# Start-up order, a second bank for the first sums of a batch, step pacing, logit order and a plain last product in a fused attention and expert kernel

## The chip, the cores and the metric

The kernel runs on one core of a Trainium2 chip. The metric is the time of one execution on the device, in microseconds (us); the time before is the median of nine runs. The engines are named as the profile names them: PE (matrix products; PEld are its weight loads), DVE (vector), ACT (scalar, with the exponential), POOL and SP; SP, ACT and POOL also issue the DMA transfers.

## The reference

Attention over 4 batches, 8 heads, 768 positions and 64 channels feeds 8 experts. A head is either a full causal one or a streaming one, which sees the first 4 positions and the last 64. The output of the attention, x, has 3072 tokens of 512 channels.

```python
mask = np.where(retr, causal, causal & (is_sink | in_win))
scores = np.where(mask, scale * (q @ k.T), -1e9)
a = softmax(scores)
x = (a @ v).transpose(0, 2, 1, 3).reshape(N, D)       # N, D = 3072, 512
P = np.exp(x @ w_gate - max)                          # N x 8
for _ in range(8):
    P /= P.sum(1, keepdims=True) + 1e-09
    P /= P.sum(0, keepdims=True) + 1e-09
    P *= N / E
out = sum(P[:, e:e + 1] * (np.maximum(x @ w1[e], 0) @ w2[e]) for e in range(8))
```

## The kernel before

**Attention, 0 to 157 us of the profiled execution.** A unit is a batch b, a block g of 256 queries (three in a batch) and a half u of the heads; a unit has two pairs of heads (a = 0, 1). `emit_prep` turns keys and queries of a unit by PE transposes into a PSUM tile "tr", which DVE copies to kT. `emit_scores` makes one chunk of scores (tile "sc", two buffers of two PSUM banks); its two closures are the exponential on ACT (L457, writes PT) and the product with a mask on DVE (L466, L469). A round is two chunks; a batch has 12 rounds: 2 with g = 0, 4 with g = 1, 6 with g = 2. `gen_pv` sums PT times v for one pair in a PSUM tile "pv" of one buffer; `normalize` (L300, L301) divides on DVE and writes xn, after which the buffer is free. `turn` transposes xn into a tile "xt", which ACT copies to xT (L319). All of tr, xt, the values' placement "vp", the logits "lgp" and the steps of expert 0 ("l1", "l2") share the PSUM tag "mo" with three buffers.

**Steps of expert 0 as filling.** Each finished query block adds six steps to the list `fillers`: four of layer 1 (`first_steps`, L355: eight products of 256 columns, counted as 1) and two of layer 2 (L369: eight of 512 columns, counted as 2), 96 counts in all. `finish_sums` puts one step between the two sums of a round, and `spend(n)` at the end of round n takes steps until a target count is reached: (with 48 rounds) 4 + 68 (n - 5) // 42. 72 are done at the last round, the other 24 go between the eight Sinkhorn iterations (L598 to L618, 157 to 181 us).

**Order.** The first six rounds are written out by hand for PE, DVE and ACT (L520 to L575: this order is kept on those engines). They begin with nine products on zeros (`keep_warm`), then `make_far` and `make_keep`, which build flags and masks from is_retrieval, then `round_first`, `emit_prep`, `scores`. After that a scheduler orders the instructions of each engine.

**Logits.** `emit_logits` makes, for a batch, 6 token blocks of 8 columns in one bank, each by four products over the channel quarters (L336), block after block.

**Experts 1 to 7, 181 us to the end.** Works are pairs (e, c) of an expert and one of six chunks of 512 tokens. Both layers use seven products in place of eight (Strassen-Winograd). `combine_h` makes four sums of hidden values for a work on DVE (L648, tile S). `layer2` takes the products in the order 1, 5, 6, 2, 7, 3, 4, each eight matmuls of 256 columns (L780), and adds each product's bank to acc: on DVE (L797) or by ACT and an accumulating DMA (L794, L802). In the last two works all adds are on DVE. `body(n)` interleaves layer 1 of a work with layer 2 of the work before; the last work's layer 2 runs after the loop alone (L858 to L860), with its banks split in halves over more PSUM tiles (`final`). `store` sends a finished quarter of a chunk by two DMAs; in the last chunk one is issued by SP and one by ACT (L761).

Of the kernel before, what the change touches and what calls it, by code (L numbers as in the profile page):

```python
# [36 lines left out]
def kernel(  # L37
# [128 lines left out]
    def round_first(h0):  # L166
# [3 lines left out]
        for i in range(2):  # L170
# [27 lines left out]
    nc.vector.memset(fm, 1.0)  # L198
    nc.vector.memset(wm, 1.0)
    retf = constp.tile([128, H], F32, tag="retf")  # L200
    nc.vector.tensor_copy(
        out=retf, in_=ret_u.rearrange("p (e two) -> p e two", two=2)[:, :, 0]
    )
    over = constp.tile([128, H], F32, tag="over")
    nc.vector.tensor_scalar(out=over, in0=retf, scalar1=-1.0, scalar2=1.0,
                            op0=ALU.mult, op1=ALU.add)
    sinks = [slice(64 * o, 64 * o + (n_sink + 1 - o) // 2) for o in range(2)]
    sinks = [rows for rows in sinks if rows.stop > rows.start]
    masks = [cp.tile([128, 2, 640], F16, tag=f"mask{j}", name=f"mask{j}") for j in range(4)]
# [3 lines left out]
    def make_keep():  # L213
        nc.vector.scalar_tensor_tensor(
            out=keep[:, 256:512], in0=wm, scalar=1.0, in1=fm, op0=ALU.add, op1=ALU.mult)
        nc.vector.tensor_copy(out=keep[:, 0:256], in_=keep[:, 256:512])
        for rows in sinks:
            nc.vector.tensor_scalar(out=keep[rows, 0:256], in0=fm[rows, :], scalar1=2.0,
                                    scalar2=None, op0=ALU.mult)
        nc.vector.tensor_copy(out=keep[:, 512:640], in_=keep[:, 256:384])  # L220
# [9 lines left out]
            )  # L230

    def make_far():

        for i in range(2):
            nc.scalar.activation(out=farf[:, :, i], in_=retf, func=AF.Copy, bias=0.0, scale=1.0)
        for rows in sinks:
            nc.vector.memset(farf[rows, :, 0], 1.0)
        for i in (1, 0):
            spell_far(i, farf[:, :, i].unsqueeze(2).broadcast_to([128, H, DV]))

# [38 lines left out]

    def gen_pv(b, g, u, a, PT, scale):  # L280

        pv = psA.tile([128, 2, 2, DV], F32, tag="pv", bufs=1, name=f"pv_{b}_{g}_{u}_{a}")
        vt, vf = vts[b], vfs.get(b)
        todo = pv_of(g)
        for i, (kj, far, sb, off) in enumerate(todo):
            for hh in range(2):
                nc.tensor.matmul(
                    out=pv[:, sb, hh, 0:D + 1], lhsT=PT[:, hh, off:off + 128],
                    rhs=(vf if far else vt)[:, 4 * u + 2 * a + hh, kj, 0:D + 1],
                    start=(i == 0 and hh == 0), stop=(i == len(todo) - 1 and hh == 1),  # L290
                    skip_group_check=True,
                )
            yield
        if a == 0:
            xns[b, g, u] = ap.tile([128, 2, 2, 2, D], F16, tag="xn", name=f"xn_{b}_{g}_{u}")
        xn = xns[b, g, u]

        def normalize():
            rc = ap.tile([128, 2, 2], F32, tag="rc", bufs=4, name=f"rc_{b}_{g}_{u}_{a}")
            nc.vector.reciprocal(out=rc, in_=pv[:, :, :, D])  # L300
            nc.vector.tensor_tensor(  # L301
                out=xn[:, a], in0=pv[:, :, :, 0:D],
                in1=rc.unsqueeze(3).broadcast_to([128, 2, 2, D]), op=ALU.mult)
            if a == 1:
                turns.append((b, g, u))
        scale.append(normalize)
# [23 lines left out]

    def emit_logits(b):
        lgp = psA.tile([128, 512], F32, tag="mo", bufs=3, name=f"lgp_{b}")
        for i in range(NC):
            nb = b * NC + i
            for dc in range(4):
                nc.tensor.matmul(  # L336
                    out=lgp[:, i * E:(i + 1) * E], lhsT=xT[dc // 2][:, dc % 2, ts(nb, 128)],
                    rhs=wg16[:, dc, :], start=(dc == 0), stop=(dc == 3),
                )
        nc.scalar.activation(  # L340
            out=Pne[:, b * NC:(b + 1) * NC, :],
            in_=lgp[:, 0:NC * E].rearrange("p (n e) -> p n e", e=E),
            func=AF.Exp, bias=0.0, scale=1.0,
        )
# [132 lines left out]
    def fill(n):  # L477

        while n > 0 and fillers:
            done = fillers.pop(0)()  # L480
            n -= done
            left[0] -= done
# [11 lines left out]

    rounds = len(tasks) // 2
    def spend(n):
        fill(left[0] - (92 - 68 * (n - 5) // (rounds - 6)))

    def sum_later(n):
        for i, a, ci in tasks[2 * n:2 * n + 2]:  # L500
# [5 lines left out]
    def scores(n):  # L506
        return [emit_scores(*t) for t in tasks[2 * n:2 * n + 2]]
# [11 lines left out]
    engines = {mybir.EngineType.PE, mybir.EngineType.DVE, mybir.EngineType.Activation}  # L519
    with tc.manual_schedule(engines=engines):  # L520
        keep_warm(blank[:, 0:128], blank, 9)
        make_far()
        make_keep()
        round_first(0)
        emit_prep(*units[0])
        round_first(4)
        r0 = scores(0)
        soften(r0, (0,))
        make_masks((0, 1))
        emit_prep(*preps.pop())  # L530
        warm(3)
        r1 = scores(1)
        soften(r1[:1], (0,))
        place_v(0)
        soften(r0, (1,))
        sum_later(0)
        soften(r1[1:], (0,))
        make_masks((2, 3))
        emit_prep(*preps.pop())
        warm(2)  # L540
        r2 = []
        finish_sums(lambda: r2.extend(scores(2)))
        soften(r1, (1,))
        soften(r2, (0,))
        warm(2)
        turn()
        sum_later(1)
        r3 = scores(3)
        place_v(1)
        finish_sums(lambda: emit_prep(*preps.pop()))  # L550
        soften(r3, (0,))
        emit_vfar(0, 1)
        soften(r2, (1,))
        sum_later(2)
        turn()
        r4 = scores(4)
        finish_sums()
        soften(r3, (1,))
        soften(r4, (0,))
        fill(1)  # L560
        sum_later(3)
        finish_sums()
        soften(r4, (1,))
        fill(1)
        r5 = scores(5)
        turn()
        emit_prep(*preps.pop())
        soften(r5, (0,))
        spell_far(2, farx[:, :, 1])
        sum_later(4)  # L570
        finish_sums()
        fill(1)
        soften(r5, (1,))
        sum_later(5)
        fill(1)  # L575
# [182 lines left out]

    def store(c, i, n):
        for o in range(2):  # L760
            (nc.scalar if c == NCH - 1 and o else nc.sync).dma_start(  # L761
                out=out[ts(c, CH), :].rearrange("(q i p c) (n d) -> i n c p q d", q=2, i=2, c=2, n=2)[i, n, o],
                in_=acc[c][64 * o:64 * o + 64, i, n, :, :],
            )

    def layer2(e, c):
        banks = {}
        final = (e, c) == works[-1]

        def product(k, bank, first, last=False):  # L770
            if first and final:

                banks[bank] = [psB.tile([128, 512], F32, tag="l1" if bank == "y" else "l2",
                                        name=f"l2{bank}{q}")[:, 0:256] for q in range(2)]
            elif first:
                t = psB.tile([128, 2, 256], F32, tag="l2", name=f"l2{bank}")
                banks[bank] = [t[:, q, :] for q in range(2)]
            for q in range(2):
                for f in range(4):
                    nc.tensor.matmul(  # L780
                        out=banks[bank][q], lhsT=lefts2[e, c][k - 1][:, q, f, :],
                        rhs=rights2[e][k - 1][:, f, :],
                        start=(first and (final or q == 0) and f == 0),
                        stop=(last and (final or q == 1) and f == 3), skip_group_check=True,
                    )

        def add(bank, i, n, by_dma):
# [23 lines left out]
        for k in (1, 5, 6, 2, 7, 3, 4):  # L811
# [5 lines left out]
                store(c, i, n)  # L817
            yield

    gens = {name: iter(()) for name in ("l1", "l2", "h", "w", "x", "first")}
# [5 lines left out]
    def body(n):  # L828
        e, c = works[n]
        if c == 0 and e + 1 < E:  # L830
            expw[e + 1] = load_expert(e + 1)
        if c == 2 and e + 1 < E:
            gens["w"] = combine_w(e + 1)
        if e == 1:
            gens["first"] = weight_first(c)
            gens["x"] = combine_x((c + 1) % NCH)
        for slot in range(7):
            go("l1", 2 if n == 0 and slot == 0 else 1)
            if slot in (1, 3):
                go("w")  # L840
                go("x", 2)
            go("l2")
            if slot in (2, 3, 5, 6):
                go("first")
            if slot in (2, 3):
                go("h")
            if n == 0 and slot == 0:
                run(combine_w(1), 9)
        gens["h"] = combine_h(e, c)
        go("h", 2)  # L850
        gens["l2"] = layer2(e, c)
        if n + 1 < len(works):
            gens["l1"] = layer1(*works[n + 1])

    with tc.manual_schedule(engines={mybir.EngineType.DVE}):
        for n in range(len(works)):
            body(n)
        for _ in range(7):  # L858
            go("h")
            go("l2")  # L860


# [33 lines left out]
```

The softmax here doesn't subtract the row's maximum and nothing guards it: scores larger than these inputs give would overflow.

## Time and profile before

| | us |
|---|---|
| median of nine runs (lowest, highest) | 707.29 (706.85, 707.64) |
| the profiled execution | 707.49 |
| its span, first to last instruction | 705.8 |
| PE, busy in the span | 686.2 |
| DVE, busy | 568.3 |
| ACT, busy | 418.0 |
| POOL, busy | 151.4 |

The time of an execution is 1.7 us longer than the span of its instructions. "Busy" counts the union of an engine's instructions; a matmul's record of 128x256 lasts 272 ns, but matmuls overlap and start about 109 ns apart. In the listings a number in brackets is the time that the engine sat idle before the instruction, with what ended the wait.

### The profile page before, as it was taken

What the parts mean: (1) busy time and instruction counts of PE and PEld (TensorE: products, weight loads), DVE (VectorE), ACT (ScalarE), POOL (GpSimd) and SP (SyncE); (2) the same over time, 40 slices, a digit from 0 to 9 for tenths busy, and PEclk for the clock granted to TensorE, in tenths of its full rate; (3) what the DMA queues carried; (4) which work ended last, traced back from release to release, by engine and by line L of the source; (5) the groups of instructions that cost most, each with busy time, mean ns of one, the idle gap of its engine ahead of it and who ended that gap; (6) DMA issues with size and microseconds to landing.
All of it is one profiled execution on the core that took longest, in us unless ns stands there. A gap on an engine that the chain in (4) does not pass through costs nothing. (4 is left out here: it accounts for less than half of the span.)

```text
span 705.8 us, 17059 instructions
## 1 busy us (share of the span) xinstructions
PE 686.2 (97%) x6932; PEld 569.2 (81%) x6932; DVE 568.3 (81%) x1157; ACT 418.0 (59%) x780; POOL 151.4 (21%) x183
## 2 busy tenths in 40 slices
PE   7999999999999999999999999999999999999995
PEld 3666666666588888888888888888888888888884
DVE  6766666757889988898888879887888789877786
ACT  6777777774795555555555555555555555555550
POOL 7432220000012131222212121222212121121210
PEclk8999999999999999999999999999999999999999
DMA  9999592000734378346924594349424944345774
GB/s 178 179 190 104 52 86 27 3 1 1 120 53 73 57 122 132 62 75 107 148 47 75 94 147 76 60 82 164 84 47 76 154 87 76 60 75 111 148 159 123
DMA packets 84223, 65.61 MB, mean 93 GB/s; under 512 B 48304, under 2 KB 64688, under 8 KB 84144
## 3 DMA queue, kind: packets, MB, share of 16 engines
q0 software_dynamic: 74976, 57.17, 58.5%
q1 hardware_dynamic: 7536, 6.30, 3.6%
q10 hardware_dynamic: 1632, 1.05, 0.5%
q8 instruction: 54, 0.88, 0.5%
q14 instruction: 25, 0.20, 0.1%
HBM read 52.45 MB, written 6.29 MB: 83 GB/s over the span
## 5 line engine op out<-in xcount | busy, mean ns | idle before, releaser
L802 POOL DMA_DIRECT2D acc<-add x120 | 101.4, 845 | 381.9 <-ACT add L794 351.4
L720 ACT ACTIVATE R<-l1y 128x512 f32<-128x512 f32 x164 | 98.7, 602 | 127.5 <-PE l1y L711 92.8
L780 PEld LDWEIGHTS <-S 128*128 128x128 f16 x1344 | 131.2, 98 | 17.0 <-DVE S L648 1.2
L711 PEld LDWEIGHTS <-S 128*128 128x128 f16 x1312 | 128.3, 98 | 17.7 <-issue 2.6
L797 DVE SCALAR_TENSOR_TENSOR acc<-l2y,Pne,acc 128x256 f32<-128x256 f32 x256 | 111.2, 475 | 29.8 <-PE l2y L780 29.7
L780 PEld LDWEIGHTS <-hT 128*128 128x128 f16 x1008 | 98.6, 98 | 12.0 <-issue 0.6
L711 PEld LDWEIGHTS <-w 128*128 128x128 f16 x984 | 96.2, 98 | 12.0 <-issue 0.6
L711 PE MATMUL l1y<-T,S 128*128 128x256 f16 x656 | 98.4, 272 | 1.8 <-ACT R L720 1.8
L457 ACT ACTIVATE PT<-sc 128x1024 f16<-128x1024 f32 (+1 forms) x96 | 83.1, 921 | 16.3 <-PE sc L448 15.4
L780 PE MATMUL l2y<-T,S 128*128 128x256 f16 x672 | 87.1, 273 | 0.0
L794 ACT ACTIVATE add<-l2w,Pne 128x256 f32<-128x256 f32 x80 | 33.7, 473 | 66.1 <-PE l2w L780 64.0
L648 DVE TENSOR_TENSOR S<-hT 128x1024 f16<-128x1024 f16 x84 | 57.6, 685 | 17.0 <-ACT hT L750 14.6
L726 DVE CUSTOM_DVE_ANT_0 hT<-l1z,R 128x512 f16<-128x512 f32 x82 | 56.2, 685 | 8.2 <-ACT R L720 8.2
L726 DVE CUSTOM_DVE_ANT_0 hT<-l1w,R 128x512 f16<-128x512 f32 x82 | 56.1, 684 | 4.3 <-PE l1w L711 0.4
L726 DVE CUSTOM_DVE_ANT_0 hT<-l1y,R 128x512 f16<-128x512 f32 x82 | 55.7, 679 | 0.1
L750 ACT ACTIVATE hT<-l1y 128x512 f16<-128x512 f32 x82 | 49.0, 597 | 4.2 <-PE l1y L711 2.8
L720 ACT ACTIVATE R<-l1w 128x512 f32<-128x512 f32 x82 | 49.4, 603 | 0.0
L711 PE MATMUL l1w<-T,S 128*128 128x256 f16 x328 | 49.4, 273 | 0.0
L711 PE MATMUL l1z<-xT,w 128*128 128x256 f16 x328 | 49.4, 273 | 0.0
L711 PE MATMUL l1w<-xT,S 128*128 128x256 f16 x328 | 49.4, 273 | 0.0
L711 PE MATMUL l1y<-T,w 128*128 128x256 f16 x328 | 49.2, 272 | 0.1
L355 PE MATMUL l<-xT,w 128*128 128x256 f16 x384 | 48.4, 272 | 0.8 <-ACT xT L319 0.8
(102 smaller groups left out, 1025.5 us busy)
## 6 DMA issues: line engine op xcount, KB each, us to landing
acc<-add POOLq DMA_DIRECT2D x120, 256.0 KB, 3.4
w<-in_moe_w_dram POOLq DMA_DIRECT2D x16, 1024.0 KB, 10.4
out_dram<-acc SPq DMA_DIRECT2D x44, 128.0 KB, 2.9
k<-in_k_dram POOLq DMA_DIRECT2D x11, 256.0 KB, 8.0
q<-in_q_dram POOLq DMA_DIRECT2D x11, 256.0 KB, 8.7
v<-in_v_dram POOLq DMA_DIRECT2D x12, 192.0 KB, 9.6
acc<-in_v_dram POOLq DMA_DIRECT2D x3, 256.0 KB, 7.7
acc<-in_q_dram ACTq DMA_DIRECT2D x2, 256.0 KB, 5.5
```

What stands on the lines that cost most here:

```text
L355: nc.tensor.matmul(out=l1[:, ts(fb % 2, 256)], lhsT=w1[:, dc, ts(fb, 128)], rhs=xT[dc // 2][:, dc % 2, c0:c0 + 256], start=(dc == 0), stop ...
L457: nc.scalar.activation(out=PT[:, :, c0:c0 + width], in_=sc[:, :, 0:width], func=AF.Exp, bias=0.0, scale=SCALE,)
L648: nc.vector.tensor_tensor(out=out_, in0=a_, in1=b_, op=op)
L711: nc.tensor.matmul(out=banks[g, bank][:, f, :], lhsT=lefts1[e][k - 1][:, dc, ts(2 * g + f, 128)], rhs=rights1[c][k - 1][:, dc, :], start=( ...
L720: nc.scalar.activation(out=R[name], in_=banks[g, bank], func=AF.Copy, bias=0.0, scale=1.0)
L726: nc.vector._custom_dve(TENSOR_ADD_SAT, out=block(g, i, n), in0=banks[g, bank], in1=R[name], s0=65504.0, s1=0.0)
L750: nc.scalar.activation(out=block(g, 1, 0), in_=banks[g, "y"], func=AF.Relu, bias=0.0, scale=1.0)
L780: nc.tensor.matmul(out=banks[bank][q], lhsT=lefts2[e, c][k - 1][:, q, f, :], rhs=rights2[e][k - 1][:, f, :], start=(first and (final or q ...
L794: nc.scalar.activation(out=t[:, q, :], in_=banks[bank][q], func=AF.Copy, bias=0.0, scale=w)
L797: nc.vector.scalar_tensor_tensor(out=dst, in0=banks[bank][q], scalar=w, in1=dst, op0=ALU.mult, op1=ALU.add,)
L802: nc.gpsimd.dma_start(out=acc[c][:, i, n, :, :], in_=t, accum_op=ALU.add)
```

## The change

Five edits in one. (1) Start-up: retf, over and farf are made inside `make_keep`, farf by DVE and not by ACT; `make_keep` comes ahead of `make_far`; the masks are made in three places, earlier; one group of three fillers of the PE's time becomes two (`warm(2)`), a second group of two is gone; the first `place_v` and the first sums are moved ahead of, or away from, `scores(1)` and `scores(2)`. (2) In `gen_pv` the sum of pair a = 1 of a block g = 0 takes a buffer of "mo". (3) `emit_logits` runs over channel quarters outside and blocks inside. (4) `spend` has a lower target for rounds 6 to 11: 5, 6, 7, 8, 9, 10 counts where it was 5, 7, 8, 10, 12, 13; from round 12 it rises by 60 counts in 35 rounds to the same 72. (5) The last work's layer 2 is plain: `layer2_last` makes four token blocks of eight matmuls of 512 columns (the last block in two halves of 256), adds each with one DVE instruction and stores it at once; `combine_h` is not called for this work, and the special banks are gone from `layer2`.

```diff
@@ make_keep (was: retf and over ahead of it, farf in make_far)
         nc.vector.tensor_copy(out=keep[:, 0:256], in_=keep[:, 256:512])
+        nc.vector.tensor_copy(
+            out=retf, in_=ret_u.rearrange("p (e two) -> p e two", two=2)[:, :, 0]
+        )
+        nc.vector.tensor_scalar(out=over, in0=retf, scalar1=-1.0, scalar2=1.0,
+                                op0=ALU.mult, op1=ALU.add)
+        for i in range(2):
+            nc.vector.tensor_copy(out=farf[:, :, i], in_=retf)
+        for rows in sinks:
+            nc.vector.memset(farf[rows, :, 0], 1.0)
@@ make_far
-        for i in range(2):
-            nc.scalar.activation(out=farf[:, :, i], in_=retf, func=AF.Copy, bias=0.0, scale=1.0)
-        for rows in sinks:
-            nc.vector.memset(farf[rows, :, 0], 1.0)
@@ gen_pv
-        pv = psA.tile([128, 2, 2, DV], F32, tag="pv", bufs=1, name=f"pv_{b}_{g}_{u}_{a}")
+        tag, bufs = ("mo", 3) if g == 0 and a == 1 else ("pv", 1)
+        pv = psA.tile([128, 512], F32, tag=tag, bufs=bufs, name=f"pv_{b}_{g}_{u}_{a}")
+        pv = pv[:, 0:4 * DV].rearrange("p (s h d) -> p s h d", s=2, h=2)
@@ emit_logits
-        for i in range(NC):
-            nb = b * NC + i
-            for dc in range(4):
+        for dc in range(4):
+            for i in range(NC):
                 nc.tensor.matmul(
...
-                    rhs=wg16[:, dc, :], start=(dc == 0), stop=(dc == 3),
+                    start=(dc == 0 and i == 0), stop=(dc == 3 and i == NC - 1),
@@ spend
-        fill(left[0] - (92 - 68 * (n - 5) // (rounds - 6)))
+        done = 4 + 8 * (n - 5) // 7 if n < 12 else 12 + 60 * (n - 12) // (rounds - 13)
+        fill(left[0] - (96 - done))
@@ the hand-written order
         keep_warm(blank[:, 0:128], blank, 9)
+        make_keep()
         make_far()
-        make_keep()
         round_first(0)
+        make_masks((0,))
         emit_prep(*units[0])
+        make_masks((1,))
         round_first(4)
         r0 = scores(0)
         soften(r0, (0,))
-        make_masks((0, 1))
+        make_masks((2, 3))
         emit_prep(*preps.pop())
-        warm(3)
-        r1 = scores(1)
-        soften(r1[:1], (0,))
+        warm(2)
         place_v(0)
         soften(r0, (1,))
         sum_later(0)
-        soften(r1[1:], (0,))
-        make_masks((2, 3))
+        r1 = scores(1)
+        soften(r1, (0,))
         emit_prep(*preps.pop())
-        warm(2)
-        r2 = []
-        finish_sums(lambda: r2.extend(scores(2)))
+        finish_sums()
+        r2 = scores(2)
@@ new
+    def layer2_last(e, c):
+        h, w2 = hTs[e, c], expw[e][1]
+        order = (4, 5, 0, 1, 2, 3, 6, 7)
+        for q, i in ((0, 0), (0, 1), (1, 0), (1, 1)):
+            pieces = 1 + (q == 1 and i == 1)
+            for n in range(pieces):
+                width = 512 // pieces
+                t = psB.tile([128, 512], F32, tag="l1" if n else "l2", name=f"last{q}{i}{n}")
...
+                for j, f in enumerate(order):
+                    nc.tensor.matmul(out=t, lhsT=h[:, q, f, ts(i, 128)],
+                                     rhs=w2[:, f, n * width:(n + 1) * width],
+                                     start=(j == 0), stop=(j == 7))
...
+                nc.vector.scalar_tensor_tensor(
+                    out=dst, in0=t.rearrange("p (n d) -> p n d", d=256),
+                    scalar=Pne[:, 4 * c + 2 * q + i, e:e + 1], in1=dst, op0=ALU.mult, op1=ALU.add)
...
+                for o in range(2):
+                    (nc.scalar if o else nc.sync).dma_start(
+                        out=rows[q, i, o][:, cols], in_=acc[c][64 * o:64 * o + 64, i, cols, q, :])
+                yield
@@ body and the loop over works
+        if n + 1 == len(works):
+            gens["l2"] = layer2_last(e, c)
+            return
...
-        for _ in range(7):
-            go("h")
-            go("l2")
+        go("l2", 9)
```

More of the change, by code (lines that the diff above doesn't have):

```diff
@@ L200 @@
     retf = constp.tile([128, H], F32, tag="retf")
-    nc.vector.tensor_copy(
-        out=retf, in_=ret_u.rearrange("p (e two) -> p e two", two=2)[:, :, 0]
-    )
     over = constp.tile([128, H], F32, tag="over")
-    nc.vector.tensor_scalar(out=over, in0=retf, scalar1=-1.0, scalar2=1.0,
-                            op0=ALU.mult, op1=ALU.add)
     sinks = [slice(64 * o, 64 * o + (n_sink + 1 - o) // 2) for o in range(2)]
@@ L332, in emit_logits @@
         lgp = psA.tile([128, 512], F32, tag="mo", bufs=3, name=f"lgp_{b}")
-        for i in range(NC):
-            nb = b * NC + i
-            for dc in range(4):
+        for dc in range(4):
+            for i in range(NC):
                 nc.tensor.matmul(
-                    out=lgp[:, i * E:(i + 1) * E], lhsT=xT[dc // 2][:, dc % 2, ts(nb, 128)],
-                    rhs=wg16[:, dc, :], start=(dc == 0), stop=(dc == 3),
+                    out=lgp[:, i * E:(i + 1) * E],
+                    lhsT=xT[dc // 2][:, dc % 2, ts(b * NC + i, 128)], rhs=wg16[:, dc, :],
+                    start=(dc == 0 and i == 0), stop=(dc == 3 and i == NC - 1),
+                    skip_group_check=True,
                 )
@@ L760, in store @@
         for o in range(2):
-            (nc.scalar if c == NCH - 1 and o else nc.sync).dma_start(
+            nc.sync.dma_start(
                 out=out[ts(c, CH), :].rearrange("(q i p c) (n d) -> i n c p q d", q=2, i=2, c=2, n=2)[i, n, o],
@@ L767, in layer2 @@
         banks = {}
-        final = (e, c) == works[-1]
         def product(k, bank, first, last=False):
[L771 to L775, printed above, removed]
+            if first:
                 t = psB.tile([128, 2, 256], F32, tag="l2", name=f"l2{bank}")
@@ L782, in product @@
                         rhs=rights2[e][k - 1][:, f, :],
-                        start=(first and (final or q == 0) and f == 0),
-                        stop=(last and (final or q == 1) and f == 3), skip_group_check=True,
+                        start=(first and q == 0 and f == 0), stop=(last and q == 1 and f == 3),
+                        skip_group_check=True,
                     )
@@ L818, in layer2 @@
             yield
+    def layer2_last(e, c):
[6 more added lines that the diff above has]
+                t = psB.tile([128, 512], F32, tag="l1" if n else "l2", name=f"last{q}{i}{n}")
+                t = t[:, 0:width]
+                for j, f in enumerate(order):
+                    nc.tensor.matmul(out=t, lhsT=h[:, q, f, ts(i, 128)],
+                                     rhs=w2[:, f, n * width:(n + 1) * width],
+                                     start=(j == 0), stop=(j == 7))
+                cols = slice(n, n + 1) if pieces == 2 else slice(0, 2)
+                dst = acc[c][:, i, cols, q, :]
+                nc.vector.scalar_tensor_tensor(
+                    out=dst, in0=t.rearrange("p (n d) -> p n d", d=256),
+                    scalar=Pne[:, 4 * c + 2 * q + i, e:e + 1], in1=dst, op0=ALU.mult, op1=ALU.add)
+                rows = out[ts(c, CH), :].rearrange("(q i p c) (n d) -> q i c p n d", q=2, i=2, c=2, n=2)
+                for o in range(2):
+                    (nc.scalar if o else nc.sync).dma_start(
+                        out=rows[q, i, o][:, cols], in_=acc[c][64 * o:64 * o + 64, i, cols, q, :])
+                yield
     gens = {name: iter(()) for name in ("l1", "l2", "h", "w", "x", "first")}
@@ L851, in body @@
         gens["l2"] = layer2(e, c)
-        if n + 1 < len(works):
-            gens["l1"] = layer1(*works[n + 1])
+        gens["l1"] = layer1(*works[n + 1])
     with tc.manual_schedule(engines={mybir.EngineType.DVE}):
```

## The prediction

> **What bounds the kernel now.** I read the page first, then the waits of PE, the timeline at both ends, and windows by stage.
>
> ```profile
> span 705.8 us, 17059 instructions
> PE 686.2 (97%) x6932; PEld 569.2 (81%) x6932; DVE 568.3 (81%) x1157; ACT 418.0 (59%) x780; POOL 151.4 (21%) x183
> ...
> 0.00:10.00 10.00, 5.29 (x33) 2.22 (x33) 5.14 (x18) 4.97 (x10) 8.62 (x17) 0.88 0.97 160
> 10.00:20.00 10.00, 9.38 (x121) 5.16 (x117) 8.05 (x22) 7.73 (x12) 4.95 (x6) 0.78 1.47 197
> 29.00:53.00 24.00, 22.70 (x321) 14.51 (x317) 15.19 (x37) 18.11 (x25) 9.83 (x11) 1.00 1.92 180
> 181.00:691.60 510.60, 508.78 (x4620) 451.63 (x4619) 438.13 (x822) 292.49 (x600) 109.89 (x130) 1.00 0.56 96
> 691.60:705.80 14.20, 6.87 (x58) 5.30 (x56) 9.04 (x21) 0.00 (x0) 0.00 (x0) 0.94 0.43 115
> ```
>
> The window rows give length, then busy time of PE, PEld, DVE, ACT and POOL, then granted clock and DMA. PE is the bound: in 181 to 691.6 us it idles 1.8 us. Its 19.6 idle us lie at the two ends (4.7 and 7.3) and in waits of the attention. The change can gain only there, since its PE work stays nearly the same. The waits, and the end:
>
> ```profile
> PE l L355 <- ACT xT L319: 0.8, 1, 0.8
> PE pv L287 <- DVE xn L301: 1.2, 5, 0.4
> ...
> 52.64 0.60 PE L355 MATMUL l<-xT,w 128*128 128x256 f16 x4 [0.84 <-ACT xT L319]
> 125.69 0.36 PE L287 MATMUL pv<-v,PT 128*128 128x65 f16 x6 [0.36 <-DVE xn L301]
> ...
> 690.96 0.60 ACT L750 ACTIVATE hT<-l1y 128x512 f16<-128x512 f32 x1 [2.79 <-PE l1y L711]
> 691.63 1.04 PE L780 MATMUL l2y<-w,hT 128*128 128x256 f16 x8
> 693.36 1.05 PE L780 MATMUL l2w<-T,S 128*128 128x256 f16 x8 [0.69 <-DVE S L648]
> 696.47 1.03 PE L780 MATMUL l2w<-w,S 128*128 128x256 f16 x8 [0.24 <-DVE acc L797]
> 698.82 1.03 PE L780 MATMUL l2y<-T,hT 128*128 128x256 f16 x8 [0.45 <-DVE acc L797]
> 699.86 0.86 DVE L797 SCALAR_TENSOR_TENSOR acc<-l2y,Pne,acc 128x256 f32<-128x256 f32 x2
> ```
>
> In the last 14 us the seven-product form makes PE wait for DVE three times; two more adds and the last stores follow.
>
> [...] eight of 256 take 0.87 us (690.76 to 691.63) and the 24 logit products of a batch 0.68 us (93.00 to 93.68), some 25 ns each plus a switch. [...] Here the clock averages 0.78 in 10 to 20 us. [...] here the output stores land 2.4 us after issue at best, 3.0 in the median.
>
> **Part 5, the plain last product.** Before: 56 matmuls of 109 ns are 6.1 us; with the waits PE ends near 699.85, DVE (two adds from 699.86) at 700.72, the last store is issued at 700.86, lands 3.3 us later (page, ACT's stores) at 704.2, and 1.6 us of semaphores and drains lead to 705.8. After: 24 matmuls of 215.7 ns and 16 of 109 are 6.92 us. They start at 691.63 too: the hidden values wanted sixth in the first block come from ACT by 691.56, those of the second token half from DVE by 691.8 (wanted 3.5 us later). Banks: the fourth l2 buffer is free, the next is freed by the adds at 692.7, wanted at 693.4. No sum by `combine_h` is waited for (four of 0.69 us leave DVE). The last matmul starts at 691.63 + 6.92 - 0.11 = 698.44; before, DVE followed the last start by 0.28 (699.58 to 699.86), so 698.72, and one add of 256 columns takes 0.47: 699.19 against 700.72, 1.5 earlier. The adds of 512 columns are not in the trace: 0.475 for 256 and 0.43 from start to start give about 0.7, under the 1.73 of a block, so they hide. The stores: ten in place of eight, at 0.6 to 0.75 us of issue on two queues, spaced by 1.73 us, so the queues are empty at the end. The last is 64 KB with one pair just ahead, where before eight of 128 KB came in 2.5 us: 2.4 to 3.3 us to land, I take 2.8, 0.5 less. Sum: 2.0 earlier (1.4 to 2.5).
>
> **Part 4, fewer steps in rounds 6 to 11.** At 52.64 PE waits 0.84 us (0.9 with the pipeline's refill) because the list is empty but for steps whose xT was only just turned. By round 11 the change has taken 3 counts less (10 for 13), so older steps are there: the instruction order after the change shows a layer 2 step at this place. What is late next: less PE work stands between rounds, and scores need their buffer back from the exponential. Walking the new order from 33.5 us with exponentials of 0.95 (1024 wide) and 0.75 from start to start: a wait of 0.3 at the second chunk of round 9, 0.2 in round 11's third, 0.3 at the first round of batch 1. The round's ACT work, 18.1 / 6 = 3.0 us, stays under its PE work, 3.4 us after the change. The counts themselves are only moved (0.87 us each, paid later, to the same 72). Gain 1.0 less 0.5: 0.5 (-0.5 to 0.9).
>
> **Part 2, the second bank.** It removes the wait of the second sum of a block g = 0 for the first one's normalize on DVE. Outside the hand-written rounds I find four: 0.17 at 88.9, 0.09 at 92.7, 0.36 at 125.3, 0.24 at 129.6, sum 0.86; the refill after each adds some 0.1. In place of it the sum holds a "mo" bank until DVE has divided (0.6 us of work), with tr, xt and a step wanting the three. Between such a sum and the third next use of "mo" the order has at least logits and scores (0.6 + 0.45) or a step (0.87): covered mostly. If the cover is gone it costs what it saved. Gain 0.7 (0 to 1.1).
>
> **Part 1, start-up.** farf by DVE after retf (4.85 + 0.52), over and two copies of about 0.2 puts the first farx copy at 6.05 where it was 5.75; ACT's first rounding starts at 7.13 and not at 6.83 (its data land just before), and the first scores at 9.7 and not 9.44: 0.3 lost. Then six mask instructions (0.40 apart) stand on DVE between the two kT copies, so the second is at 12.1 and not 11.3; `place_v` needs its bank, 12.85; its ACT copies, 1.1, now come ahead of the exponentials of round 1, which end at 16.1. That is when those of round 2 started before (16.08). From there the paths meet: the second pair of scores of round 3 waits for that exponential (17.85; was 17.98). The second bank spares 0.25 at 16.4, the masks for round 1 run 0.3 earlier, and at 20.8 xn on DVE is 0.1 earlier. PE loses three idle-time fillers (0.43 each cold), which were idle time. Gain 0.1. [...] I take 0 (0.4 to -0.7).
>
> **Part 3, logits.** Already at 25 ns a product, with each block's four products on one place. [...] the waits on xT at 157 us stay, since the last eight products still need the last xT. 0.
>
> **Sum.** 2.0 + 0.5 + 0.7 + 0 + 0 = 3.2. The scheduler also puts the later steps at other places in batches 1 to 3; their remaining waits (0.50 on xn at 100, 0.24 at 136, 0.29 on PT at 144) may grow or go, counted 0. The profiled execution, 707.49 with a span of 705.8, becomes 704.3; it lay 0.20 over the median of its runs, 707.29, so the median becomes 704.1.
>
> **Rivals.** *Only the end gains*: the attention's waits move elsewhere (part 4 and part 2 give back what they take). For it: PE's work is the same and every bank and buffer is in use. Against: the 0.84 and the four xn waits have named causes that go. 707.29 - 2.0 = 705.3. *Cold start*: [...] 705.0. For it: three fillers less. [...] *All better*: stores land at 2.4, batches 1 to 3 lose two of their remaining waits, start-up wins 0.4: 703.0. *Slower*: the second bank starves "mo". In batches 1 to 3 six sums hold a bank until DVE has divided, and where DVE is late the next tr, xt or step stops PE. At one division a sum (reciprocal 0.18 and product 0.42) that is 6 x 0.6 = 3.6 us, with part 2's 0.7 not gained: 707.29 - 2.0 - 0.5 + 3.6 = 708.4. It decides from (2.0 + 0.5) / 6 = 0.42 us a sum. For it: the bank is held longest where DVE is late, which is where the waits were. Against: the third next use of "mo" comes over 0.9 us later, and the trace shows hardly a PE wait for a bank of "mo" now.
>
> **How the numbers follow.** Forecast 704.1 at 0.51; only the end, 705.3, 0.20; cold start, 705.0, 0.13; all better, 703.0, 0.10; slower, 0.06. The range: the unknown costs reach from 702.8 (just past the all-better case) to 705.9 (only the end, with its low value 1.4). A measurement of this kernel can tell 0.2%, 1.4 us, from no change: faster is under 705.9. That takes the forecast, all better, and most of only the end and cold start: 0.86; within 0.08; slower 0.06.
>
> **What would show it.** After the change: the last DVE add ends some 6.5 us before the span's end and 7.6 after the last work's first matmul, with no PE wait on S or acc; no wait of a step on xT near 50 us; no pv on xn in the later batches; first scores at 9.7; logits still 0.6 to 0.7 us a batch. Wrong if PE's idle time in 22 to 157 us doesn't fall by about 1 us, if the clock stays halved past 14.5 us, or if the last stores land later than 3.3 us after issue.

## The result and the profile after

Nine runs of the changed kernel have a median of 703.14 us (702.13 to 703.49) beside 707.24 for 29 runs of the kernel before; the ratio is 0.9941 (95% interval 0.9933 to 0.9950), so about 4.2 us or 0.6% faster. In a later set of five runs the ratio was 0.9938 (0.9926 to 0.9950). The forecast was 704.1 in a range of 702.8 to 705.9: right in direction and range, 1.0 us short in size. The profiled execution after took 702.45 us, at the low end of its runs, and the one before 707.49, a little over its median; so their spans differ by 5.0, and I take sizes from stretches of the traces rather than from the two spans.

The page after, its first two lines:

```profile
span 700.7 us, 17004 instructions
PE 685.8 (98%) x6913; PEld 568.2 (81%) x6913; DVE 564.2 (81%) x1147; ACT 416.6 (59%) x777; POOL 151.4 (22%) x183
```

PE's work is the same to 0.4 us, and its idle time fell from 19.6 to 14.9 us. Windows by stage of the kernel after (length, then busy time of PE, PEld, DVE, ACT, POOL, then clock and DMA):

```profile
10.00:20.00 10.00, 8.71 (x120) 4.87 (x116) 7.84 (x22) 8.21 (x13) 4.02 (x5) 1.00 1.47 197
181.00:689.50 508.50, 506.87 (x4611) 450.67 (x4610) 436.14 (x818) 291.01 (x598) 109.92 (x130) 1.00 0.56 95
689.50:700.70 11.20, 7.14 (x42) 3.87 (x40) 4.30 (x8) 0.00 (x0) 0.00 (x0) 0.95 0.58 147
```

The clock of 1.00 in the first of these rows is not to be set beside the 0.78 of before: this trace has no record of the clock ahead of a switch to full at 13.49 us, and its matmuls are slow until then. Eight transposes of the same kind, before and after the switch:

```profile
10.36 0.64 PE L254 MATMUL tr<-ident,k 128*64 128x128 f16 x8
...
13.66 0.41 PE L254 MATMUL tr<-ident,k 128*64 128x128 f16 x8
```

The last stretch, from the last work's first matmul, has shrunk from 14.1 to 11.2 us, with DVE's work more than halved. Its timeline after, in part:

```profile
688.88 0.60 ACT L756 ACTIVATE hT<-l1y 128x512 f16<-128x512 f32 x1 [2.79 <-PE l1y L717]
689.55 7.09 PE L833 MATMUL last<-w,hT 128*128 128x512 f16 x40
...
691.48 0.75 DVE L838 SCALAR_TENSOR_TENSOR acc<-last,Pne,acc 128x512 f32<-128x512 f32 x1 [0.85 <-PE last L833]
...
693.21 0.75 DVE L838 SCALAR_TENSOR_TENSOR acc<-last,Pne,acc 128x512 f32<-128x512 f32 x1 [0.98 <-PE last L833]
...
696.68 0.48 DVE L838 SCALAR_TENSOR_TENSOR acc<-last,Pne,acc 128x256 f32<-128x256 f32 x1 [0.39 <-PE last L833]
```

Forty matmuls stand in one row without a bracket: no wait for DVE is left, and now DVE waits for PE. In the attention I compare PE's waits by what ended them (total us, times, longest) between 22 and 157.5 us. Before:

```profile
PE l L355 <- ACT xT L319: 0.8, 1, 0.8
PE pv L287 <- DVE xn L301: 0.8, 3, 0.4
PE sc L448 <- ACT PT L457: 0.7, 3, 0.3
PE xt L316 <- DVE xn L301: 0.7, 2, 0.5
PE lgp L336 <- ACT xT L319: 0.3, 1, 0.3
PE pv L287 <- DVE PT L469: 0.2, 1, 0.2
```

After:

```profile
PE sc L453 <- ACT PT L462: 1.4, 5, 0.3
PE xt L319 <- DVE xn L304: 0.3, 1, 0.3
PE lgp L339 <- ACT xT L322: 0.3, 1, 0.3
PE pv L290 <- ACT xT L322: 0.2, 1, 0.2
PE pv L290 <- DVE PT L474: 0.2, 1, 0.2
```

The two waits that the change aims at, sums on xn and a step on xT, are gone. The waits of scores on the exponential have doubled. PE's idle time in these 135.5 us fell from 3.63 to 2.55 us (busy 131.87 before, 132.95 after), about the 1 us that the prediction had named.

### The profile page after: what moved, and what is told of

Its sections match the earlier page's. It is cut to its first block, busy times and chain, and to the rows that moved or that the text cites. A ratio compares the mean times of both kernels' runs of the same rounds, so it can differ in the third digit from the quotient of the medians.

```text
span 700.7 us, 17004 instructions
## 1 busy us (share of the span) xinstructions
PE 685.8 (98%) x6913; PEld 568.2 (81%) x6913; DVE 564.2 (81%) x1147; ACT 416.6 (59%) x777; POOL 151.4 (22%) x183
## 3 DMA queue, kind: packets, MB, share of 16 engines
q10 hardware_dynamic: 1648, 1.05, 0.6%
## 4 chain that ended last, share of the span: by engine, by line
PE 62%; ACT 0%; DVE 0%; issue 0%
PE l1y L717 17%; PE l2y L781 17%; PE l2w L781 9%; PE l1w L717 9%; PE l2z L781 4%; PE l1z L717 4%; PE last L833 1%; ACT R L726 0%; DVE acc L838 0%
## 5 line engine op out<-in xcount | busy, mean ns | idle before, releaser
L717 PEld LDWEIGHTS <-S 128*128 128x128 f16 x1312 | 128.3, 98 | 17.5 <-issue 2.4
L781 PEld LDWEIGHTS <-S 128*128 128x128 f16 x1312 | 128.1, 98 | 15.3 <-DVE S L654 0.2
L798 DVE SCALAR_TENSOR_TENSOR acc<-l2y,Pne,acc 128x256 f32<-128x256 f32 x248 | 107.7, 475 | 29.9 <-PE l2y L781 29.8
L781 PEld LDWEIGHTS <-hT 128*128 128x128 f16 x984 | 96.3, 98 | 11.2
L781 PE MATMUL l2y<-T,S 128*128 128x256 f16 x656 | 85.0, 273 | 0.0
L717 PE MATMUL l1y<-xT,w 128*128 128x256 f16 x328 | 49.2, 273 | 0.0
```

The lines of the kernel that those rows point to most:

```text
L717: nc.tensor.matmul(out=banks[g, bank][:, f, :], lhsT=lefts1[e][k - 1][:, dc, ts(2 * g + f, 128)], rhs=rights1[c][k - 1][:, dc, :], start=( ...
L781: nc.tensor.matmul(out=banks[bank][q], lhsT=lefts2[e, c][k - 1][:, q, f, :], rhs=rights2[e][k - 1][:, f, :], start=(first and q == 0 and f ...
L798: nc.vector.scalar_tensor_tensor(out=dst, in0=banks[bank][q], scalar=w, in1=dst, op0=ALU.mult, op1=ALU.add,)
```

## The experiments

The traces let me cut each profiled execution at five points. In the table, "round 4" is the start of that round's first scores, "attention" the time from there to the Sinkhorn stage's first matmul (L609, after L615), "experts" from there to the first matmul of the last work's layer 2, "adds" from there to the end of DVE's last add, and "close" from there to the end of the span. All are differences of start and end times in the traces, in us.

| kernel | round 4 | attention | experts | adds | close |
|---|---|---|---|---|---|
| before | 21.07 | 138.59 | 531.97 | 9.09 | 5.05 |
| after | 20.39 | 137.31 | 531.85 | 7.61 | 3.58 |
| after, again | 20.55 | 137.31 | 531.50 | 7.61 | 3.58 |
| end alone | 21.07 | 138.62 | 532.28 | 7.62 | 3.56 |
| pacing alone | 20.87 | 139.03 | 532.66 | 9.09 | 4.95 |
| bank alone | 20.97 | 137.25 | 532.73 | 9.10 | 5.01 |
| start-up alone | 21.43 | 138.62 | 532.36 | 9.09 | 5.01 |
| logits alone | 20.74 | 138.61 | 532.49 | 9.10 | 4.87 |
| after without start-up | 20.55 | 137.31 | 532.66 | 7.62 | 3.48 |
| after without pacing | 20.57 | 137.25 | 532.35 | 7.61 | 3.60 |
| after without pacing, again | 20.18 | 137.25 | 531.71 | 7.61 | 3.58 |
| after without bank | 20.41 | 139.03 | 531.86 | 7.62 | 3.56 |
| last block in one piece | 20.66 | 137.31 | 531.65 | 7.86 | 4.47 |
| late stores | 20.26 | 137.32 | 531.88 | 7.61 | 5.76 |

Between kernels whose code is the same there, the columns attention and adds repeat to within 0.03 us and close to within 0.2; they follow the code. The columns round 4 and experts vary by up to 1.0 (21.43 and 20.41, start-up alone and after without bank) and 1.2 us between such kernels; they carry the scatter of the times.

### One part at a time, on the kernel before

Each kernel is the kernel before with one of the diff's five parts as shown.

**The end** (`layer2_last`, `body`, the loop over works, `store`, `layer2`):

> The kernel before with the plain last product alone. Theory A (the end was undervalued: the last stores land sooner than I allowed, as the changed kernel's trace with 3.5 us from the last add to the span's end against 5.0 has it): 2.8 to 3.0 us faster, last work's first matmul to the span's end 11.1 to 11.3 us. Theory B (the end gives the 2.0 us of the prediction and the rest comes from the start and the attention): 1.8 to 2.2 us faster, that stretch 12.0 to 12.3 us.

Measured 704.38 us against 707.58, ratio 0.9956 (0.9944 to 0.9969): 3.1 us faster. Adds and close together fall from 14.14 to 11.18. Theory A holds: the end is worth 3.0 us, of which 1.47 is in the adds, as predicted, and 1.49 in the close, where I had 0.5.

**The pacing**:

```diff
-        fill(left[0] - (92 - 68 * (n - 5) // (rounds - 6)))
+        done = 4 + 8 * (n - 5) // 7 if n < 12 else 12 + 60 * (n - 12) // (rounds - 13)
+        fill(left[0] - (96 - done))
```

> The kernel before with the lower step target of rounds 6 to 11 alone. Prediction: 0.5 us faster, the wait of a step on xT near 51 us gone, new waits of scores on the exponential of some 0.5 us in 33 to 48 us. Theory A (attention gains as predicted, 1.2 us in all with the bank): 0.3 to 0.8 us faster. Theory C (the pacing alone makes the whole gain of the attention): 1.0 to 1.4 us faster.

Measured 707.85 against 707.58, ratio 1.0004 (0.9996 to 1.0013): no gain, and in the trace the attention is 0.44 us longer. PE's waits in 22 to 157.5 us with pacing alone:

```profile
PE sc L448 <- ACT PT L457: 1.4, 5, 0.3
PE pv L287 <- DVE xn L301: 1.0, 3, 0.4
PE xt L316 <- DVE xn L301: 0.3, 1, 0.3
PE l L355 <- ACT xT L319: 0.2, 1, 0.2
```

The wait on xT near 52 us is gone, as forecast; the 0.2 in the last row is another one, at 87 us. But PE, arriving sooner at the first sums of batch 1, now waits there for DVE, and later rounds wait for the exponential. The first of these, in the timeline with pacing alone:

```profile
50.82 0.36 PE L287 MATMUL pv<-v,PT 128*128 128x65 f16 x6 [0.36 <-DVE xn L301]
```

**The second bank**:

```diff
-        pv = psA.tile([128, 2, 2, DV], F32, tag="pv", bufs=1, name=f"pv_{b}_{g}_{u}_{a}")
+        tag, bufs = ("mo", 3) if g == 0 and a == 1 else ("pv", 1)
+        pv = psA.tile([128, 512], F32, tag=tag, bufs=bufs, name=f"pv_{b}_{g}_{u}_{a}")
```

> The kernel before with the second sum of a block g = 0 in a shared bank alone. Prediction: 0.7 us faster, no sum waiting for xn in batches 1 to 3. Theory C (pacing does it all): 0 to 0.2. If the shared bank starves others (the rival on the slow side): slower by 1 us or more, with PE waits of tr, xt or steps on a DVE or ACT result near 56, 93 and 128 us.

Measured 705.89 against 707.58, ratio 0.9974 (0.9963 to 0.9984): 1.8 us faster (1.1 to 2.6), 1.34 of it in the attention stretch of the trace; the interval of the times does not part the two. None of the three expectations had that much. PE's waits in 22 to 157.5 us with the bank alone:

```profile
PE l L358 <- ACT xT L322: 0.8, 1, 0.8
PE sc L451 <- ACT PT L460: 0.7, 3, 0.3
PE xt L319 <- DVE xn L304: 0.7, 2, 0.5
PE lgp L339 <- ACT xT L322: 0.3, 1, 0.3
PE pv L290 <- DVE PT L472: 0.2, 1, 0.2
```

The row of sums on xn is gone and every other row is as before: nothing was given back, and the starving of "mo" didn't come. How 0.86 us of waiting (the four brackets, the smallest of which is too short for this list) can be worth 1.34 is seen at one place. Before, timeline:

```profile
123.45 1.89 PE L369 MATMUL l<-w,hT 128*128 128x512 f16 x8
125.69 0.36 PE L287 MATMUL pv<-v,PT 128*128 128x65 f16 x6 [0.36 <-DVE xn L301]
```

With the bank:

```profile
122.69 1.89 PE L372 MATMUL l<-w,hT 128*128 128x512 f16 x8
124.42 0.35 PE L290 MATMUL pv<-v,PT 128*128 128x65 f16 x6
```

From the step to the sum took 2.24 us and takes 1.73, 0.51 less, where the bracket says 0.36. The record of a matmul lasts longer (0.38 us at 512 columns) than the distance to the next start (0.216), and the bracket counts from the record's end. So a wait costs its bracket and some 0.16 us more (the eight matmuls above are 7 x 0.216 + 0.38 = 1.89). In the changed kernel's trace the first 24 matmuls of the last work, each with its own weights, start 215 to 216 ns apart too. For the four waits brackets and 0.16 each make 1.5, a little more than the 1.34 measured. Matched at the matmuls that both traces have in the same order, the two traces part by 0.34, 0.26, 0.53 and 0.16 us at the four waits, whose brackets are 0.17, 0.09, 0.36 and 0.24. So the working holds at three of them. At the last one less was won than the bracket says.

**The start-up order**, with the sums still in one bank:

> The kernel before with the new start-up order alone, sums still in one bank. Prediction: 0 (0.4 faster to 0.7 slower). Theory A: 0.3 to 0.7 us faster, since the changed kernel reached the first scores of round 4 0.68 us earlier (20.39 against 21.07). Theory D ([...] full clock from 13.49 and not 14.49 us): 0 within 0.3 over several runs.

Measured 707.56 against 707.58, ratio 0.9996 (0.9988 to 1.0004): nothing, as predicted and as theory D has it. That the moment of full clock sets the start of round 4, which is theory D's reason, is not shown: the kernel with late stores below, which has the new start-up too, got full clock only from 15.04 us and began round 4 at 20.26.

**The logits' order**:

```diff
-        for i in range(NC):
-            nb = b * NC + i
-            for dc in range(4):
+        for dc in range(4):
+            for i in range(NC):
```

> The kernel before with the new order of the logit products alone. Prediction: 0, the products at 25 ns from start to start as before, 24 in 0.6 to 0.7 us; from round 4 to the Sinkhorn stage 138.6 us. A gain of 0.3 us or more would say that products on one place did stall.

Measured 707.48 against 707.44, ratio 1.0000 (0.9992 to 1.0008). Timeline of the first batch's logits with this edit alone:

```profile
55.80 0.75 PE L336 MATMUL lgp<-wg,xT 128*128 128x8 f16 x24
56.48 0.28 PE L450 MATMUL sc<-kT,kT 64*128 64x256 f16 x2
```

24 products take 0.68 us, to the hundredth what they took before in the prediction's example, and in both traces the median distance of their starts is 25 ns. In the trace of before the next product starts 0.10 us after the last of the 24.

### One part taken out of the changed kernel

**Without the new start-up order:**

> The changed kernel with the old start-up order. Theory D (the new order is worth nothing by itself, 0.3 faster with an interval over zero when alone): as the changed kernel, 703.1 to 703.9, that is 0.0 to 0.5 behind it. Theory E (the new order and the second bank help each other, because the two first sums then follow each other without a division between): 0.6 to 1.0 us behind the changed kernel, and the first scores of round 4 at 20.8 to 21.1 us.

Measured 703.49 (703.29 to 703.68), ratio to before 0.9939 (0.9924 to 0.9953), where the changed kernel has 0.9941 and 0.9938. No loss; round 4 starts at 20.55, as in the changed kernel's second trace. Theory D again, and not theory E.

**Without pacing, twice:**

> The changed kernel with the old step target. Alone the pacing gave 0.3 us slower (nothing, by its interval): in its trace the wait on xT near 51 us was gone, but waits of sums on xn at 50 and 54 us and of scores on the exponential at 80 us had come. Theory F (those sums' waits are what the second bank removes, so that in the changed kernel pacing is worth the predicted 0.5 or more): 0.5 to 1.0 us behind the changed kernel. Theory G (the steps are only moved, and new waits come whatever the bank): within 0.3 us of it or ahead of it.

> The changed kernel with the old step target, to be compared with the changed kernel on one chip. Theory G (pacing only trades its waits): the same within 0.4 us, since the stretch from round 4 to the Sinkhorn stage took 137.25 us in its trace and 137.31 in the changed kernel's. Theory J (pacing costs, and the version without it is the best one): 0.6 to 1.2 us ahead of the changed kernel, as the two ratios of separate runs to the kernel before have it (0.9925 and 0.9941).

The first set gave 702.58 us with a ratio of 0.9925 (0.9911 to 0.9939) and looked like a version that beats the change. The second set, beside the changed kernel on one chip, gave 703.31 against 703.27, ratios 0.9940 (0.9927 to 0.9953) and 0.9938. So no better version is shown: theory G, with 0.06 us between them in the attention stretch. That its old wait is back and still costs nothing overall is plain from the second trace of this kernel:

```profile
50.53 0.38 PE L360 MATMUL l<-xT,w 128*128 128x256 f16 x2
51.75 0.81 PE L360 MATMUL l<-xT,w 128*128 128x256 f16 x6 [0.84 <-ACT xT L322]
```

In exchange, waits of the changed kernel are absent from it, such as these two of the changed kernel's timeline:

```profile
60.16 0.28 PE L319 MATMUL xt<-ident,xn 128*128 128x128 f16 x2 [0.34 <-DVE xn L304]
...
79.06 0.34 PE L453 MATMUL sc<-kT 64*128 64x256 f16 x4 [0.34 <-ACT PT L462]
```

**Without the second bank:**

> The changed kernel with one bank for the sums again. If the parts add up as they did alone (bank 1.8 us): 1.8 us behind the changed kernel. Theory E (bank, start-up order and pacing need each other: without the bank the new start-up order reached round 4 at 21.43 us and pacing lengthened the attention by 0.43): 2.4 to 2.9 us behind it, first scores of round 4 at 21.2 to 21.5, and waits of sums on xn back at 50, 54, 88, 92, 125 and 129 us.

Measured 704.90, ratio 0.9968 (0.9959 to 0.9978), against 703.27: 1.6 us behind by the medians, 2.1 by the ratios. The attention stretch is 1.72 longer, which is the bank's 1.34 and the 0.38 by which pacing is worse without it. The waits on xn came back, ahead of sums at 50.4, 54.1, 87.5, 125.8 and 130.0 us. But round 4 began at 20.41 and not at 21.2 or later, so theory E fails as to the start-up: it needs the bank to no visible extent.

### The stores at the end

**The last block in one piece**, so that the last pair of stores has 128 KB each:

```diff
-            pieces = 1 + (q == 1 and i == 1)
+            pieces = 1
```

> The changed kernel with the last token block in one piece of 512 columns, so that the last add takes 0.75 us in place of 0.48 and the last two stores have 128 KB. Theory H (a store lands sooner because few are under way): span from the last add's end to the end still 3.5 to 3.7 us, so 0.3 us slower in all. Theory I (it lands sooner because it is small): 3.9 to 4.3 us, 0.7 to 1.0 us slower in all.

**The output in the old quarters**, four stores of 128 KB issued together after the last add (stores of the first quarters after the block before it):

```diff
-                for o in range(2):
-                    (nc.scalar if o else nc.sync).dma_start(
-                        out=rows[q, i, o][:, cols], in_=acc[c][64 * o:64 * o + 64, i, cols, q, :])
+                if q == 1 and n + 1 == pieces:
+                    for m in range(2):
+                        for o in range(2):
+                            (nc.scalar if o else nc.sync).dma_start(
+                                out=out[ts(c, CH), :].rearrange(
+                                    "(q i p c) (n d) -> i n c p q d", q=2, i=2, c=2, n=2)[i, m, o],
+                                in_=acc[c][64 * o:64 * o + 64, i, m, :, :])
```

> The changed kernel with the last chunk's output stored in the old quarters, each when both token halves are added: four stores of 128 KB are issued together after the last add, two on each queue. Theory H (few under way): from the last add's end to the span's end 4.6 to 5.0 us as in the kernel before, 1.1 to 1.5 us slower in all. If only the second issue of 0.6 us on each queue counts: 4.1 to 4.2 us, 0.6 us slower.

Measured 703.93 us (ratio 0.9945, 0.9931 to 0.9959) and 704.76 (0.9957, 0.9943 to 0.9971), so 0.3 to 0.5 and 1.1 to 1.3 us behind the changed kernel, by its ratios of 0.9941 and 0.9938. These are four runs each, with intervals of 1 us to either side. In the traces adds and close together are 1.14 and 2.18 us longer, which such intervals do not exclude; I go by the traces. The close was 4.47 and 5.76 where 3.58 is the changed kernel's, and both are longer than any theory had. The time from issue to landing of the last chunk's stores, minimum, median and maximum, in the changed kernel, in one piece, and with late stores, one line each:

```profile
DMA to landing us min/median/max: 2.3/2.6/2.8
```

```profile
DMA to landing us min/median/max: 2.5/2.8/2.9
```

```profile
DMA to landing us min/median/max: 2.6/3.2/3.4
```

The last store of all took 3.31 us before, 2.33 after, 2.84 in one piece, 3.26 with late stores. So with few under way a 128 KB store lands 0.47 us sooner (2.84 for 3.31), which is theory H's part. The layout is not the cause: late stores have the old one, and their first pair, with nothing just ahead of it, landed in 2.59 and 2.84. Another 0.51 goes with the half size, theory I's part, but size alone is not what counts: in the trace of before, 12 of the 48 stores of 128 KB, all sent by SP with no other store issued at the same moment, landed in 2.38 to 2.42, less than 0.1 above the 64 KB store. An equal store of 128 KB issued at the same moment costs more than that: of such a pair in one piece the first landed in 2.50 and the second in 2.84. With late stores the last store was also issued later, 0.89 us after the last add and not 0.19, behind another one on its queue.

A third share I had not thought of: from the last landing to the end of the span SP's and POOL's closing waits took 1.60 us before, 1.60 in one piece and 1.62 with late stores, but 1.06 in the changed kernel. All fourteen traces fall into these two groups, 1.05 to 1.10 in the seven with 64 KB stores at the end and 1.59 to 1.62 in the other seven. SP takes its closing waits one after the other, and in every trace one pause of some 0.43 us stands between two of them. Where the last stores are 64 KB it lies ahead of the last landing, which covers it (699.00 to 699.44 us in the changed kernel's second trace, last landing 699.49); in the others it comes after (704.36 to 704.79 before, last landing 704.17). What SP waits for there, and why the place differs, the traces don't name; that stays open.

## Why the prediction was right, and where not

The bound was read rightly: PE's work hardly changed and the gain is PE's idle time at the end and in the attention. By its steps:

*Part 5, the end, 2.0 predicted, 3.0 measured.* The adds' share is exact: 1.5 predicted, 1.48 measured (9.09 to 7.61), last add 7.6 us after the first matmul as written down, the add of 512 columns 0.75 us where 0.7 was estimated. The mis-sized term is the close: I took 2.8 us to land and an unchanged closing of 1.6; they are 2.33 and 1.06. (The 6.5 us from the last add to the span's end among the signs was a slip: the forecast's own terms, 699.19 and 705.8 - 2.0, give 4.6; it was 3.58.) The quiet stores here took 2.3 for 64 KB and 2.4 for 128, a pair of 128 KB 2.5 and 2.8, the crowded ones 3.3. I took a value between the quiet and the crowded, although the trace of before has 12 stores at 2.4.

*Part 4, the pacing, 0.5 predicted, about 0 measured* (-0.06 with the bank, -0.44 without, both from the attention stretch). The step "what is late next" failed. I walked the new order only as far as the rounds whose target falls and the first of batch 1 (with exponentials of 0.95 and 0.75 us from start to start, which in the trace of before start 0.90 and 0.69 apart where ACT does not wait), and named waits of 0.3, 0.2 and 0.3 there. Already the sum was wrong: these make 0.8, of which I took off only 0.5, and the wait of 0.9 to be gained became 1.0; 0.9 - 0.8 is 0.1, close to what was measured. But that would have been luck, since of the three waits only one of 0.07 came, in round 11. The steps taken out were put into the later batches and the scheduler placed the others anew. So two older waits of PE on xn went as well, 0.50 near 100 and 0.24 near 136 us, and against these and the 0.84 stand seven new ones of 1.39 in all, the largest ahead of 60, 79 and 114 us.

*Part 2, the bank, 0.7 predicted, 1.34 measured in the attention and 1.8 (1.1 to 2.6) in time.* The mechanism was right and the rival on the slow side, the starved "mo", is excluded. The gain also lies outside its range of 0 to 1.1. Two terms were mis-sized. The 0.1 us a wait for the refill, an estimate, was 0.12 on the mean of the four (1.34 less 0.86). The allowance for giving back was not needed: 0.86 and four refills of 0.1 make 1.26, from which I took off more than 0.5. Also, part 4 and part 2 were off in opposite directions: together I had 1.2, and the attention stretch fell by 1.28. The sum was right there by luck of that kind.

*Part 1, the start-up, 0 predicted, 0 measured* (ratio 0.9996 alone). First scores came at 9.60, forecast 9.7. The rival "cold start" has full clock come later because PE has fewer fillers, and -0.7 as the low end of the range rests on that; it was an assumption of mine. (Before, the granted clock was 0.50 from 10 to 14.4 us and 1.00 from 14.5 to 20; near 11.5 us matmuls of 512 columns started 0.42 us apart, at full clock 0.216.) It isn't seen: full clock came between 12.65 and 15.05 us in the eight traces with the new start-up and between 13.02 and 14.72 in the six with the old one, so the latest of the eight is 0.33 us behind the latest of the six. A later full clock may have come elsewhere: of the 13 runs without the bank the three with the lowest mean clock, 0.989, 0.990 and 0.993, were the longest, 707.8, 706.7 and 706.4 us, against 704.0 to 705.9 for those at 0.995 or more. Only one of the 13 was traced, so where these three lost their time is not shown.

*Part 3, the logits, 0 and 0.* The traces show 25 ns from start to start in both orders, so products on one place did not stall. That no other order would go below 25 ns is not shown.

*The sum.* 3.2 predicted; 3.0 + 1.28 + 0 = 4.3 from the traces, 4.2 from the ratio. Of the rivals, "all better" (703.0) lies nearest in time, and nearer than the forecast, but only a part of its mechanism came: the stores landed sooner and two of the remaining waits went, but others took their place, and the start-up won nothing. It was the landing and the closing that made it.

## What to carry to other kernels

At a kernel's end count to the landing and past it: a last store that is small and with few others under way was worth 1.0 us here (2.33 us to land for 3.31), and with the pause of SP that it covers 1.5, as much as the shorter computation. A wait in the profile can cost PE more than its bracket (0.51 us for 0.36 at the wait shown above), by the part of the last matmul's record that would have been overlapped; compare starts with starts. And an edit that only moves filling work must be followed to where the work goes: removing a visible 0.84 us wait gained nothing, because the same time was lost in smaller waits elsewhere.

## What was not expected of the hardware

Stores of 128 KB issued at the same moment on SP's and ACT's queues landed 0.3 us apart: 2.50 us for SP and 2.82 for ACT in the changed kernel's second and third pair. It goes with the order and not with the queue: in the first pair ACT's issue ended first (692.98 and 693.00 us), and ACT's store landed 0.29 us ahead of SP's.

The attention stretch repeats to within 0.03 us between executions of kernels with the same code there, while the expert stretch of the same code varied from 531.5 to 532.7; the scatter of the times comes from there and from the start-up. A good part of it is one event: in five of the fourteen traces PE waited once near 265 us, for 0.61 to 0.93 us, because ACT had waited 1.22 to 1.54 us for the landing of an accumulating DMA. Why that DMA landed late in these five is not shown.
